# Top-k attention and a gated MLP on one core: low words and signs ahead of the copy of values in ScalarE's queue

## The chip, the cores and the metric

The kernel runs on one core of one Trainium2 chip. A core has a tensor engine (PE in the profile, with its weight loads as PEld), VectorE (DVE), ScalarE (ACT), GpSimd (POOL) and SyncE (SP, which issues the transfers here). Each engine works through its own queue in program order, and semaphores tie the queues together. The metric is the device time of one execution in microseconds, as the median of several runs.

## The reference

```python
# q, k, v: (8, 8, 576, 64) float32; w_in: (512, 2048), w_out: (2048, 512)
scores = scale * np.matmul(q, k.transpose(0, 1, 3, 2))          # (8, 8, 576, 576)
kth = np.partition(scores, -32, axis=-1)[..., -32:-31]
scores = np.where(scores >= kth, scores, -1000000000.0)
attn = np.exp(scores - np.max(scores, axis=-1, keepdims=True))
attn = attn / (np.sum(attn, axis=-1, keepdims=True) + 1e-09)
x = np.matmul(attn, v)            # then (B, H, S, D) -> (4608, 512)
h = x @ w_in
g = h * (1.0 / (1.0 + np.exp(-1.702 * h)))
out = (g @ w_out).astype(np.float32)
```

Every row of scores keeps its 32 largest entries, goes through a softmax and is multiplied by the values. The result goes through two matrix products with a quick GELU between them.
The weights arrive as 64-bit floats: each is one low and one high 32-bit word.

## The kernel before

The work is cut into 144 *slots*; a slot is 128 rows of two heads. Slot n runs a pipeline over neighbouring slots: top-k of slot n on VectorE, the exponentials of slot n-1 on ScalarE, the transposes ("turn") and the products with the values of slot n-2 on PE, and the scores of slot n+2 on PE.

The weights are brought in as 32 pieces of 128 x 512 in the first twelve slots (0 to 11). Each is rebuilt from its two words by five steps on three engines:

```python
raws = pool("raws", 8)            # pieces land here, eight buffers
dgp = pool("dgp", 1)              # diagonals "by", one buffer
ps_t = pool("ps_t", 2, space=PSUM)  # transposes (tp) and values (o) share two buffers

def finish():                     # GpSimd, in the slot behind the piece's own
    nc.gpsimd.tensor_tensor(out=whole, in0=whole, in1=low.bitcast(I32), op=ALU.add)      # L140
    nc.gpsimd.tensor_tensor(out=dst, in0=dst, in1=high, op=ALU.mult)                     # L141
return {
    "size": lambda: nc.scalar.activation(dst, high, AF.Abs, scale=REBASE),               # L144
    "shift": lambda: nc.vector.tensor_scalar(bits, bits, 3, None, op0=ALU.logical_shift_left),  # L145
    "sign": lambda: nc.scalar.activation(high, high, AF.Sign),                           # L146
    "low": lambda: nc.scalar.mul(out=low.bitcast(I32), in_=low, mul=2.0**-29),           # L147
    "finish": finish,
}
```

The fillers are products of the identity that nobody reads. They keep PE busy while there is no MLP work:

```python
def stay_warm(count, of=ident[:]):
    none = ps_p.tile([P, C], F32, name="none", tag="po")
    for i in range(count):
        nc.tensor.matmul(none[:, 0:P], lhsT=of, rhs=of, start=True, stop=True)           # L162
```

One of the first twelve slots in program order (cut; each engine's queue is what it gets of this, in this order):

```python
def slot(n):
    # ... loads for later slots
    some = [round_piece(x) for x in by_slot.get(n, [])] if n else early
    # ... (slot 0 does low and sign here)
    bounds(n - 1)                 # GpSimd: cut, low (L270, L271)
    exponentials(n - 1)           # ScalarE: two Prelu (L279), two Exp (L281), sums into den
    copy_scores(n + 1)            # ScalarE: sc out of PSUM (L242)
    tanh(False)                   # ScalarE, if an MLP block waits (L402)
    if n > 1:
        turn_main(n - 2)          # PE: tp (L312), ScalarE: pt (L320), twice
        turn_ends(n - 2)          # PE: tp (L315), ScalarE: pt
    for piece in some:
        piece["size"]()
    for i, op in enumerate(topk(n)):      # VectorE: eight MAX8 (L251), six MATCH_REPLACE8 (L254)
        op()
        if i == 2:
            for _ in range(min(2, len(unfinished))):
                finish_one()      # GpSimd: two pieces of the slot before
        if i == 5:
            if n > 0:
                divide(n - 1)     # VectorE: some (L290), rden (L292); GpSimd: by (L296), twice
            while unfinished:
                finish_one()      # GpSimd: the pieces left over
        if i == 9:
            gate(False)           # VectorE (L418)
    for piece in some:
        piece["shift"]()
        unfinished.append(piece["finish"])
    if n > PROJECTS and may_project(2):   # PROJECTS = 7
        project(range(G))         # PE: po, four fp32 products (L433), eight rows in the profile
    # ... prepare in slots 0 to 3
    scores(n + 2)                 # PE: s_ps (L231)
    # ...
    idle = not ready and n < PROJECTS
    if idle and n > 1:
        stay_warm(4)
    if n > 1:
        values(n - 2)             # PE: o (L342), ScalarE: xT (L354)
    for piece in some:
        piece["low"]()
    # ... prepare in later slots
    for piece in some:
        piece["sign"]()
    if idle:
        stay_warm(4)
    hidden()                      # PE: one MLP block, ph (L385), if one is ready
```

The slots from 12 on have another order (two at a time), and no pieces and no fillers. The change doesn't touch them.

Of the kernel before, what the change touches and what calls it, by code (L numbers as in the profile page):

```python
# [28 lines left out]
def kernel(  # L29
# [94 lines left out]
    def round_piece(n):  # L124

        c, g = pieces[n]
        dst = wout[:, g, :] if c is None else win[:, c, g * PIECE : (g + 1) * PIECE]
        words = raw.pop(n)[:].rearrange("p (n w) -> p n w", w=2)
        low, high = words[:, :, 0], words[:, :, 1].bitcast(F32)
        bits, whole = dst.bitcast(U32), dst.bitcast(I32)

        def finish():
# [10 lines that stand above are left out]
# [8 lines left out]
# [5 lines that stand above are left out]
# [75 lines left out]
    def copy_scores(n):  # L238
        ps = st[n].pop("ps")
        sc = st[n]["sc"] = scp.tile([P, 2, S], F32, name="sc")  # L240
        for i in range(2):
            nc.scalar.copy(out=sc[:, i, :].rearrange("p (c k) -> p c k", c=2), in_=ps[i][:, :, 0:HALF])  # L242

    def topk(n):

        sc = st[n]["sc"]
        top = st[n]["top"] = small.tile([P, 2, TOPK], F32, name="top")
        left = lefts.tile([P, 2, S], F32, name="left")

        def largest(r, i):  # L250
            nc.vector.max(top[:, i, 8 * r : 8 * r + 8], (left if r else sc)[:, i, :])  # L251

        def remove(r, i):
            nc.vector.match_replace(  # L254
                left[:, i, :], top[:, i, 8 * r : 8 * r + 8], (left if r else sc)[:, i, :], LOWEST
            )

        ops = []
        for r in range(TOPK // 8):
            ops += [lambda r=r, i=i: largest(r, i) for i in range(2)]  # L260
            if r < TOPK // 8 - 1:
                ops += [lambda r=r, i=i: remove(r, i) for i in range(2)]
        return ops

    def bounds(n):

        top = st[n]["top"]
        cut = st[n]["cut"] = small.tile([P, 2], F32, name="cut")
        low = st[n]["low"] = small.tile([P, 2], F32, name="low")
        nc.gpsimd.tensor_scalar(cut[:], top[:, :, TOPK - 1], -1.0, None, op0=ALU.mult)  # L270
        nc.gpsimd.tensor_tensor(out=low[:], in0=top[:, :, TOPK - 1], in1=top[:, :, 0], op=ALU.subtract)  # L271

    def exponentials(n):

        sc, cut, low = st[n]["sc"], st[n]["cut"], st[n]["low"]
        pr = st[n]["pr"] = prp.tile([P, 2 * S], F32, name="pr")
        den = st[n]["den"] = small.tile([P, 2], F32, name="den")
        for i in range(2):
            nc.scalar.activation(sc[:, i, :], sc[:, i, :], AF.Prelu, bias=cut[:, i : i + 1], alpha=HUGE)  # L279
        for i in range(2):  # L280
            nc.scalar.activation(  # L281
                pr[:, i * S : (i + 1) * S], sc[:, i, :], AF.Exp, bias=low[:, i : i + 1],
                accum_out=den[:, i : i + 1],
            )

    def divide(n):

        den, pr = st[n]["den"], st[n]["pr"]
        some = small.tile([P, 2], F32, name="some")
        nc.vector.tensor_scalar_add(some[:], den[:], 1e-9)  # L290
        rden = small.tile([P, 2], F32, name="rden")
        nc.vector.reciprocal(rden[:], some[:])  # L292
        if n < SETTLED:
            by = st[n]["by"] = dgp.tile([P, 2, P], F32, name="by")
            for i in range(2):
                nc.gpsimd.tensor_scalar(by[:, i, :], ident[:], rden[:, i : i + 1], None, op0=ALU.mult)  # L296
        else:
            nc.scalar.activation(pr[:, 0:S], pr[:, 0:S], AF.Copy, scale=rden[:, 0:1])
            nc.gpsimd.tensor_scalar(pr[:, S : 2 * S], pr[:, S : 2 * S], rden[:, 1:2], None, op0=ALU.mult)  # L299
# [22 lines left out]
    def turn_main(n):  # L322
        for i in range(2):
            turn(n, i * NF, MAIN[i], NF)

    def turn_ends(n):

        turn(n, 2 * NF, FULL, 1)
# [68 lines left out]
    def tanh(aside):  # L397

        if to_gate:
            ph, g, rows = to_gate.pop()  # L400
            th = thp.tile([P, G, P], F32, name="th")
            nc.scalar.activation(th[:], ph[:], AF.Tanh, scale=0.851 / RAISE)  # L402
            if aside:
                h = raws.tile([P, G, P], F32, name="h", tag="raw")
                nc.scalar.copy(out=h[:], in_=ph[:])
                ph = h
            gated.append((th, ph, g, rows))

    def gate(aside):
        if not gated:  # L410
            return
        th, h, g, rows = gated.pop()
        gT = gtp.tile([P, G, P], F32, name="gT")
        if aside:
            nc.gpsimd.tensor_scalar(th[:], th[:], 1.0, None, op0=ALU.add)  # L415
            nc.gpsimd.tensor_tensor(out=gT[:], in0=th[:], in1=h[:], op=ALU.mult)  # L416
        else:
            nc.vector.scalar_tensor_tensor(  # L418
                out=gT[:], in0=th[:], scalar=1.0, in1=h[:], op0=ALU.add, op1=ALU.mult
            )  # L420
        to_project.append((gT, g, rows))
# [29 lines left out]
    READY = (((-9, -8), (-7, -6), (-4, -3), (-2, -1)), ((-7, -6), (-4, -3), (-3, -2), (-1, -2)))  # L451
    FETCH = (((-13, -12), (-11, -10), (-7, -7), (-5, -4)), ((-11, -10), (-9, -8), (-5, -5), (-2, -2)))
    VALUES = ((-8, -7, 0, 0), (-8, -7, 2, 2))
    by_slot = dict(enumerate([2, 2, 2, 3, 3, 3, 3, 4, 3, 3, 2, 2]))
    for n in by_slot:
        first = sum(map(len, list(by_slot.values())[:n]))
        by_slot[n] = list(range(first, first + by_slot[n]))
# [19 lines left out]
    def finish_one():  # L477
        unfinished.pop(0)()
        finished.append(None)

    def may_project(waiting):

        return len(to_project) > waiting and len(finished) >= NG * CC + (to_project[0][1] + 1) * G
# [25 lines left out]
    def slot(n):  # L509

        todo = later.pop(n, [])
        for fn, args in todo:
            if fn is not prepare:
                fn(*args)
        preparing = [args for fn, args in todo if fn is prepare]
        some = [round_piece(x) for x in by_slot.get(n, [])] if n else early
        if n == 0:
# [3 lines that stand above are left out]
        else:  # L521
            bounds(n - 1)
            exponentials(n - 1)
            copy_scores(n + 1)
            tanh(False)
            if n > 1:
                turn_main(n - 2)
                turn_ends(n - 2)
            for piece in some:
                piece["size"]()  # L530
        for i, op in enumerate(topk(n)):
# [3 lines that stand above are left out]
                    finish_one()  # L535
            if i == 5:
                if n > 0:
                    divide(n - 1)
                while unfinished:
                    finish_one()  # L540
            if i == 9:
                gate(False)
# [3 lines that stand above are left out]
        if n > PROJECTS and may_project(2):  # L546
            project(range(G))
        if n < NP:
            for args in preparing:
                prepare(*args)  # L550
        scores(n + 2)
        if n == SETTLED:
            copy_scores(n + 2)
        if n == 0:
            return
        idle = not ready and n < PROJECTS
        if idle and n > 1:
            stay_warm(4)
        if n > 1:
            values(n - 2)  # L560
        for piece in some:
            piece["low"]()
        if n >= NP:
            for args in preparing:
                prepare(*args)
        for piece in some:
            piece["sign"]()
        if idle:
            stay_warm(4)
        hidden()  # L570

    def last_slot():
# [115 lines left out]
```

## Time and profile before

The time before is 1635.64 us (median of 3 runs, 1635.34 to 1639.87). The profiled execution has a span of 1639.6 us.

| engine | busy us | share of the span |
|---|---|---|
| PE (matmul) | 1590.0 | 97% |
| PEld (weight load) | 1185.1 | 72% |
| DVE | 1474.0 | 90% |
| ACT | 1153.8 | 70% |
| POOL | 750.7 | 46% |

The shares are averages over two stages. Up to about 173 us the twelve slots with pieces run; behind them come the slots that are all attention and MLP. The engines are read stage by stage below.

How to read the views: a row of the timeline or of the chain of waits begins with its start and its duration in us, then come the engine, the line of the kernel, the operation and the tiles (out<-in). "xN" is a count; an fp32 product shows as two rows, so four fillers are "x8". Text in square brackets is idle time ahead of a row and what ended it. Durations of following rows overlap a little, so a step's cost is taken from start to start. The list of waits gives "who <- whom: us in total, times, longest".

### The profile page before, as it was taken

The numbers are of one execution on the slowest core, as the hardware profiler recorded it, in microseconds if no ns is written. First come the engines' busy times: TensorE is split into PE (matmuls) and PEld (weight loads), VectorE is DVE, ScalarE is ACT, GpSimd is POOL, SyncE is SP. The second block draws the span as 40 slices with busy tenths as digits, with TensorE's granted clock in tenths as the row PEclk, the third lists the DMA queues.
The fourth block names the chain that finished last, engine by engine and source line by source line (L and its number), as shares of the span: only waits on it lengthen the run. The fifth ranks groups of instructions, "written<-read, shape, count | busy, mean of one in ns | idle before, by whom it ended". The sixth has DMA issues, their size and how long they took to land.

```text
span 1639.6 us, 32136 instructions
## 1 busy us (share of the span) xinstructions
PE 1590.0 (97%) x12031; PEld 1185.1 (72%) x12031; DVE 1474.0 (90%) x3213; ACT 1153.8 (70%) x2446; POOL 750.7 (46%) x782
## 2 busy tenths in 40 slices
PE   7678999999999999999999999999999999999999
PEld 5466677777777777777777777777777777777776
DVE  7887899999999999999999998999999999999960
ACT  6786776777777777777777777677777777777761
POOL 3676444444444444444444444444444444444430
PEclk7789999999999999999999999999999999999999
DMA  7232001110001001111000100111000100000000
GB/s 240 93 129 81 22 22 29 29 43 15 23 15 43 23 22 29 29 28 30 13 21 12 37 22 22 30 29 43 15 23 15 44 22 22 22 8 8 8 7 14
DMA packets 100636, 56.61 MB, mean 35 GB/s; under 512 B 83584, under 2 KB 91776, under 8 KB 100480
## 3 DMA queue, kind: packets, MB, share of 16 engines
q1 hardware_dynamic: 100480, 54.55, 11.7%
q8 instruction: 95, 1.56, 0.4%
q14 instruction: 61, 0.50, 0.1%
HBM read 45.09 MB, written 9.44 MB: 33 GB/s over the span
## 4 chain that ended last, share of the span: by engine, by line
PE 91%; ACT 5%; DVE 2%; issue 1%; POOL 0%; DMA 0%; SPq 0%; POOLq 0%; ACTq 0%
PE ph L385 31%; PE po L433 30%; PE s_ps L231 10%; PE o L342 10%; PE tp L310 8%; PE tp L199 2%; ACT sc L242 1%; ACT pr L281 1%; ACT raw L147 1%; ACT raw L146 1%; DVE top L251 1%; DVE left L254 1%; ACT sc L279 0%; PE none L162 0%; PE tp L315 0%
## 5 line engine op out<-in xcount | busy, mean ns | idle before, releaser
L251 DVE MAX8 top<-left 128x8 f32<-128x576 f32 x864 | 609.4, 747 | 0.0
L433 PE MATMUL po<-wout,gT 128*128 128x512 f32 x1152 | 545.2, 598 | 1.9 <-POOL wout L141 1.2
L385 PEld LDWEIGHTS ph<-xT,win 128*128 128x128 f32 x4096 | 467.4, 192 | 40.1 <-issue 39.8
L385 PE MATMUL ph<-xT,win 128*128 128x128 f32 x4096 | 484.5, 277 | 0.0
L254 DVE MATCH_REPLACE8 left<-top,left 128x576 f32<-128x576 f32 x576 | 423.3, 743 | 0.0
L299 POOL TENSOR_SCALAR pr<-pr,rden 128x576 f32<-128x576 f32 x133 | 230.1, 1730 | 348.2 <-ACT th L402 348.2
L433 PEld LDWEIGHTS po<-wout,gT 128*128 128x128 f32 x1152 | 199.1, 192 | 150.1 <-issue 143.3
L415 POOL TENSOR_SCALAR th<-th 128x512 f32<-128x512 f32 x132 | 197.4, 1495 | 228.1 <-ACT th L402 228.1
L320 ACT COPY pt<-tp 128x512 f32<-128x512 f32 (+1 forms) x432 | 193.0, 482 | 149.4 <-PE tp L310 142.7
L279 ACT ACTIVATE sc<-sc,cut 128x576 f32<-128x576 f32 x288 | 208.1, 774 | 116.0 <-POOL cut L270 116.0
L281 ACT ACTIVATE pr<-sc,low 128x576 f32<-128x576 f32 x288 | 219.2, 764 | 0.0
L242 ACT COPY sc<-s_ps 128x576 f32<-128x576 f32 x288 | 169.7, 644 | 69.2 <-PE s_ps L231 69.0
L310 PEld LDWEIGHTS tp<-ident,pr 128*128 128x128 f32 x1197 | 143.2, 141 | 101.9 <-issue 57.2
L254 DVE MATCH_REPLACE8 left<-top,sc 128x576 f32<-128x576 f32 x288 | 211.6, 742 | 0.0
L251 DVE MAX8 top<-sc 128x8 f32<-128x576 f32 x288 | 202.1, 743 | 10.1 <-ACT sc L242 10.1
L231 PE MATMUL s_ps<-k_t,q_t 64*128 64x288 f32 (+1 forms) x1280 | 187.0, 439 | 1.1 <-ACT k_t L201 1.0
L310 PE MATMUL tp<-ident,pr 128*128 128x128 f32 x1197 | 174.1, 273 | 0.0
L416 POOL TENSOR_TENSOR gT<-th,h 128x512 f32<-128x512 f32 x132 | 168.7, 1278 | 11.0
L342 PE MATMUL o<-pt,v_l 128*64 128x128 f32 (+1 forms) x2560 | 159.0, 267 | 0.7
L342 PEld LDWEIGHTS o<-pt,v_l 128*64 128x64 f32 x2560 | 131.6, 138 | 31.9 <-ACT pt L320 13.5
L231 PEld LDWEIGHTS s_ps<-k_t,q_t 64*128 64x128 f32 (+1 forms) x1280 | 101.4, 181 | 63.1 <-issue 43.6
L290 DVE TENSOR_SCALAR some<-den 128x2 f32<-128x2 f32 x144 | 46.3, 322 | 102.2 <-ACT pr L281 102.2
(55 smaller groups left out, 1164.1 us busy)
## 6 DMA issues: line engine op xcount, KB each, us to landing
q_l<-in_q_dram SPq DMA_DIRECT2D x64, 128.0 KB, 2.9
k_l<-in_k_dram SPq DMA_DIRECT2D x64, 128.0 KB, 2.9
raw<-in_moe_w_in_dram SPq DMA_DIRECT2D x16, 512.0 KB, 5.1
v_l<-in_v_dram SPq DMA_DIRECT2D x32, 256.0 KB, 2.9
raw<-in_moe_w_out_dram SPq DMA_DIRECT2D x16, 512.0 KB, 3.3
out_dram<-ob SPq DMA_DIRECT2D x32, 256.0 KB, 2.3
ends<-in_q_dram SPq DMA_DIRECT2D x32, 32.0 KB, 2.4
ends<-in_k_dram SPq DMA_DIRECT2D x32, 32.0 KB, 2.5
```

The source lines that it names most:

```text
L231: nc.tensor.matmul(ps[i][rows, c, 0:HALF], lhsT=qT[b, hps[p]][on, cols], rhs=kT[b, hps[p]][on, FIRST[i] + c * HALF : FIRST[i] + (c + 1) * ...
L251: nc.vector.max(top[:, i, 8 * r : 8 * r + 8], (left if r else sc)[:, i, :])
L254: nc.vector.match_replace(left[:, i, :], top[:, i, 8 * r : 8 * r + 8], (left if r else sc)[:, i, :], LOWEST)
L279: nc.scalar.activation(sc[:, i, :], sc[:, i, :], AF.Prelu, bias=cut[:, i : i + 1], alpha=HUGE)
L281: nc.scalar.activation(pr[:, i * S : (i + 1) * S], sc[:, i, :], AF.Exp, bias=low[:, i : i + 1], accum_out=den[:, i : i + 1],)
L299: nc.gpsimd.tensor_scalar(pr[:, S : 2 * S], pr[:, S : 2 * S], rden[:, 1:2], None, op0=ALU.mult)
L310: nc.tensor.transpose(tp[:, c * P : (c + 1) * P], pr[:, at], ident[:])
L320: nc.scalar.copy(out=to, in_=tp[:, 0 : blocks * P])
L342: nc.tensor.matmul(o[j * D : (j + 1) * D, 0 : cols.stop - cols.start], lhsT=main[:, j, c, :] if c < NF else tail[:, j, :], rhs=pt[:, j * N ...
L385: nc.tensor.matmul(ph[:, i, :], lhsT=win[:, c, f * P : (f + 1) * P], rhs=xT[:, c, :], start=(c == 0), stop=(c == CC - 1),)
L415: nc.gpsimd.tensor_scalar(th[:], th[:], 1.0, None, op0=ALU.add)
L433: nc.tensor.matmul(po[:], lhsT=gT[:, i, :], rhs=wout[:, f, :], start=(f == 0), stop=(f == FC - 1))
```

## The change

Three things change, all in the first twelve slots.

- The low words and the signs of a slot's pieces are issued ahead of values, so in ScalarE's queue they stand ahead of the copy of values (xT), which has to wait for PE. Before, they stood behind it.
- The fillers of PE that stood half ahead of values and half behind it now all stand behind it. (In slot 1, which had only the four behind, there are eight.)
- The pieces are spread anew: slot 2 rounds three in place of two, and slot 7 three in place of four.

```diff
-    by_slot = dict(enumerate([2, 2, 2, 3, 3, 3, 3, 4, 3, 3, 2, 2]))
+    by_slot = dict(enumerate([2, 2, 3, 3, 3, 3, 3, 3, 3, 3, 2, 2]))
@@ slot(n) @@
             return
+        for piece in some:
+            piece["low"]()
+        for piece in some:
+            piece["sign"]()
         idle = not ready and n < PROJECTS
-        if idle and n > 1:
-            stay_warm(4)
         if n > 1:
             values(n - 2)
-        for piece in some:
-            piece["low"]()
         if n >= NP:
             for args in preparing:
                 prepare(*args)
-        for piece in some:
-            piece["sign"]()
         if idle:
-            stay_warm(4)
+            stay_warm(8)
         hidden()
```

The aim is that ScalarE does work that needs nothing from PE while it would otherwise wait for PE, and that values, and with them the next slot's exponentials, come earlier. No arithmetic on the data changes.

## The prediction

> **What bounds the kernel now.** I first read the busy shares and the clock row of the page. Over the whole span the tensor engine is 97% busy, so the question was whether the change touches a stretch where it is not. The pieces of weights are rounded in the first twelve slots only (slots 0 to 11), so I cut the span at the starts of ScalarE's first Prelu in slots 1 and 12 (20.57 and 173.08 us in its timeline). The view of stretches (length; busy PE, PEld, DVE, ACT, POOL; granted clock; DMA share; GB/s):
>
> ```profile
> 20.57:173.08 152.51, 115.42 (x821) 89.06 (x819) 126.56 (x279) 115.27 (x233) 99.62 (x105) 0.84 0.37 123
> 180.30:1639.60 1459.30, 1455.06 (x11132) 1082.98 (x11132) 1329.63 (x2895) 1020.81 (x2174) 641.93 (x660) 1.00 0.09 24
> ```
>
> From 180 us on PE is busy 1455 of 1459 us at full clock: nothing that the change does can shorten that part. In the head no engine is full: DVE, the fullest, works 126.6 of 152.5 us, and PE runs at 0.84 of its clock. So the head is a chain through engines. The chain of waits in slots 3 and 4 shows its links (start, us, engine and tile):
>
> ```profile
> 53.64 0.27 ACT xT L354
> 53.90 1.73 ACT raw L147 x3
> 55.63 1.67 ACT raw L146 x3
> 57.30 0.71 ACT sc L279 x2
> 58.01 0.51 issue
> 58.52 1.63 ACT pr L281 x4
> 60.15 1.06 ACT sc L242 x2
> 61.20 0.49 ACT pt L320
> 61.69 0.04 issue
> 61.74 0.69 PE tp L315 x4
> 62.43 2.22 PE s_ps L231 x8
> 64.65 2.00 PE none L162 x8
> 66.66 1.32 PE o L342 x20
> 67.97 0.02 issue
> 68.00 0.27 ACT xT L354
> ```
>
> Read it as a ring. The copy of values (xT) waits for values (o) on PE. Low words (L147) and signs (L146) stand behind it in ScalarE's queue, though they need nothing from PE. Then come Prelu and Exp, the copies of scores and of pt, and PE again, where four fillers (none) stand ahead of values. One round: 57.30 to 71.67 (the next sc L279 in the chain) is 14.37 us. The list of waits from 40 to 175 us says who sits idle for it (total us, times, longest):
>
> ```profile
> PE tp L315 <- ACT pt L320: 32.6, 9, 5.3
> ACT xT L354 <- PE o L342: 31.6, 8, 6.3
> DVE some L290 <- ACT pr L281: 25.6, 8, 5.1
> ```
>
> ScalarE idles 31.6 us ahead of the copy of values while the low words and signs could run. DVE idles 25.6 us for the exponentials' sums. DVE's own timeline gives what a slot costs it:
>
> ```profile
> 51.44 1.08 DVE L145 TENSOR_SCALAR win<-win 128x512 uint32<-128x512 uint32 x3
> 60.18 0.17 DVE L290 TENSOR_SCALAR some<-den 128x2 f32<-128x2 f32 x1 [3.56 <-ACT pr L281]
> 122.46 3.37 DVE L145 TENSOR_SCALAR wout<-wout 128x512 uint32<-128x512 uint32 x3
> ```
>
> Three shifts take 1.0 us (the next instruction starts at 52.44), and once 3.37 us, while GpSimd works on wout.
>
> **What the Trainium skill says.** "TensorE: Matmul & The Clock Gate", section "Architectural detail: the array is 16× 32×32, not 1× 128×128", calls ScalarE, VectorE and GpSimd strict FIFO. The trace agrees: low words issued behind xT start only after it (53.80 after 53.64), after 4.25 us of idleness. The same page, "What's actually happening", says that an idle window of about 3.4 us halves PE's clock and a busy one restores it. The trace agrees roughly: in slots 3 to 7, behind idle gaps of 2.2 to 5.3 us, eight score matmuls take 2.2 us; behind the gap of 1.94 us at 165 us they take 1.17. "SBUF — State Buffer", section "Who interferes with whom", says that DVE's tensor_scalar in its two-port mode and GpSimd block each other; the 3.37 us above fit that.
>
> **The change, part by part.**
>
> *Order in ScalarE's queue.* For a slot with three pieces the ring loses 1.73 + 1.67 = 3.40 us, since low and sign now run while PE does L315, scores and values. They add no work. ScalarE's own content of a slot becomes its limit: Prelu start to the third pt copy 57.19 to 62.64 = 5.45, sizes 1.72, low 1.73, sign 1.67, xT 0.2: 10.8 us, and 11.3 with the tanh (0.49), from slot 6 on.
>
> *Fillers.* Four fillers ahead of values go: 2.00 us of the ring in slots 2 to 4, somewhat less in slot 5. Eight now follow values. In slot 1 there are eight where four were, at a half-cold clock some 1 to 2 us more of PE. There PE has about 1 us to spare before pt is wanted at 35.06, so I charge 0.2.
>
> *The ring after both.* 14.37 - 3.40 - 2.00 = 8.97 us, shorter than the other limits, so it ceases to bind. What binds instead, for three pieces: DVE: top-k 9.91 (30.95 to 40.86) + shifts 1.00 = 10.9, with the gate (0.59) 11.5. ScalarE 10.8 or 11.3. GpSimd: bounds 0.84, three finishes of 1.37 + 1.26 each 7.9, the two diagonals 1.16: 9.9. So DVE binds, with ScalarE right behind.
>
> *Pieces.* With four pieces slot 7's finishes would keep GpSimd 12.5 us, above DVE; three keep it at 9.9. Slot 2 takes the third piece: ScalarE there ends at about 42.0, as Prelu of slot 3 did (42.16), so it is free. Its load is issued at about 25 us and wanted at 37.5.
>
> *Slots 8 to 10* also hold eight projecting matmuls ahead of scores and values on the ring. Before: 16.65, 16.77 and 15.68 us, with po at 4.9 to 5.4 us because PE had just idled. Minus low and sign (3.4): 13.2. If PE stays warm, its whole content is L315 0.44, po 3.44 (the tail's x8 rows), scores 1.17, values 1.27, ph 3.6, transposes 1.78: 11.7 us, a full engine. I take 12.2 for slot 8 (part cold) and 11.8 for slot 9. In slot 10 the last projecting matmul needs the third finish of slot 9's pieces, which stands behind the diagonals: Prelu + 5.4, + 1.2, + 2.6, + last matmul 0.9, + scores, values and xT 2.7 = 12.8.
>
> The sum, as distances between Prelus of following slots, before and after:
> slot 1 10.57, 10.6; slot 2 11.02, 10.9; slot 3 15.03, 10.9; slot 4 14.37, 11.0; slot 5 14.09, 11.1; slot 6 13.04, 11.8 (DVE 11.5, and the first ph block, which now waits for the late xT copy, pushes transposes by 0.3); slot 7 14.36, 11.7; slot 8 16.65, 12.2; slot 9 16.77, 11.8; slot 10 15.68, 12.8; slot 11 10.93, 11.2 (DVE 9.91 + 0.59 + 0.66).
> Totals 152.5 and 126.0: 26.5 us less. Behind slot 12 PE is full and its work is the same, so this carries to the end: 1635.64 - 26.5 = 1609.1. I add 1 us for frictions: 1610.
>
> **The rivals.** *DVE and GpSimd collide.* Without gaps both are near full, and the shifts may fall on finishes each time: 1.1 us each in place of 0.34, 2.3 us a slot. Against it: GpSimd's 9.9 leaves it a gap of 1 us, which falls where the next top-k ends. If it happens in half of nine slots, +10 us: 1620. *PE stays cold or binds in slots 6 to 10.* With fillers behind values, and ph behind fillers, transposes come later; if po stays at 4.9, slots 8 to 10 cost 13.2 each: +3 us, 1613. *The head's gain is absorbed later*, because PE then waits for DVE or for weights. Against it: DVE is 91% busy behind 180 us and PE had waited there for nothing; the finishes come earlier as well. It would leave 1625 or more; I give it little. *More than my sum:* DVE's gaps (25.6) and its stretched shifts (2.4) are nearly all that the head can give, about 29 us with no stall at all: 1606.5.
>
> **Range and chances.** The floor near 1606 is hard, as DVE's work stays; 0.3 us more in each of nine slots is 1613, 0.8 is 1617. So 1605 to 1617. Two per cent would be 32.7 us, more than DVE's gaps hold: 0.05 for faster by over 2%. Slower by 2% needs a new wait of 60 us: 0.01.
>
> **What would show it.** Right: the waits of DVE on pr and of ScalarE on o fall from 25.6 and 31.6 us to a few; Prelus of slots 3 to 5 stand 10.9 to 11.2 us apart; slot 12's first Prelu starts at about 147; the clock of the head rises above 0.9; the part behind it keeps its length. Wrong: DVE idle for GpSimd or shifts of over 2 us (collision), po at 4.9 us (cold), or PE gaps behind 160 us that were not there.

## The result, and the profile after

The changed kernel takes 1616.31 us (median of 4 runs, 1614.26 to 1616.51). The kernel before, timed with it, takes 1637.76 us (4 runs, 1635.34 to 1641.75). The ratio is 0.9864, with a 95% interval of 0.9839 to 0.9889: 21.4 us less, between 18 and 26 by the interval. The forecast was 1610 us, with a range of 1605 to 1617.

The view of stretches of the changed kernel, cut at the same places as before, the first Prelu of slot 1 and of slot 12 (columns: length; busy PE, PEld, DVE, ACT, POOL; clock; DMA share; GB/s):

```profile
21.80:149.09 127.29, 106.80 (x824) 84.68 (x822) 123.82 (x280) 115.39 (x233) 101.89 (x106) 0.89 0.45 146
156.30:1614.70 1458.40, 1454.20 (x11131) 1082.50 (x11129) 1328.76 (x2893) 1020.88 (x2174) 640.92 (x660) 1.00 0.09 24
```

The head fell from 152.5 to 127.3 us and DVE now works 123.8 of them, 97%. The stretch behind it is as long as it was (1458.4 for 1459.3 us), at full clock and full of PE. The gain was made in the head, and nothing took it back later. In the two traces the first Prelu of slot 1 comes 1.2 us later, slots 1 to 11 take 25.2 us less and slot 12 0.9 us less; together that is the 24.9 us between these two executions (1641.35 and 1616.48 us).

The list of waits from 40 to 149 us has the three rows that carried the prediction, much smaller:

```profile
PE tp L315 <- ACT pt L320: 14.0, 5, 3.6
ACT xT L354 <- PE o L342: 6.7, 3, 3.8
DVE some L290 <- ACT pr L281: 3.0, 2, 2.1
```

ScalarE's waits for values fell from 31.6 to 6.7 us, DVE's for the exponentials from 25.6 to 3.0. The chain of waits of slots 3 and 4 no longer goes round through ScalarE and PE:

```profile
43.18 1.32 DVE top L251 x2
44.49 1.46 DVE left L254 x2
45.95 1.33 DVE top L251 x2
47.28 0.08 DVE some L290
47.36 0.02 issue
47.38 0.15 DVE rden L292
47.53 1.46 DVE left L254 x2
48.99 1.32 DVE top L251 x2
50.31 1.46 DVE left L254 x2
51.77 1.33 DVE top L251 x2
53.09 1.00 DVE win L145 x3
54.09 1.32 DVE top L251 x2
```

One slot of VectorE without a gap: 43.18 to 54.09 is 10.91 us. From slot 8 on PE takes over: its timeline shows no idle time from 104.12 us, ahead of slot 8's projecting matmuls, to 133 us, ahead of the last one of slot 10. The distances between the first Prelus of following slots (read from ScalarE's timeline) compare step by step with the forecast. "Again" is a second execution of the changed kernel, from the runs below.

| slot | before | forecast | changed | again |
|---|---|---|---|---|
| 1 | 10.57 | 10.6 | 10.58 | 10.57 |
| 2 | 11.02 | 10.9 | 10.91 | 11.21 |
| 3 | 15.03 | 10.9 | 10.92 | 10.68 |
| 4 | 14.37 | 11.0 | 10.91 | 10.85 |
| 5 | 14.09 | 11.1 | 10.91 | 10.91 |
| 6 | 13.04 | 11.8 | 12.04 | 11.51 |
| 7 | 14.36 | 11.7 | 10.98 | 11.51 |
| 8 | 16.65 | 12.2 | 13.46 | 11.73 |
| 9 | 16.77 | 11.8 | 11.97 | 11.97 |
| 10 | 15.68 | 12.8 | 13.46 | 13.44 |
| 11 | 10.93 | 11.2 | 11.15 | 11.14 |
| sum | 152.5 | 126.0 | 127.3 | 125.5 |

### The profile page after: what moved, and what is told of

It reads as the page before. It is cut to its first block, busy times and chain, and to the rows that moved or that the text cites. A ratio compares the mean times of both kernels' runs of the same rounds, so it can differ in the third digit from the quotient of the medians.

```text
span 1614.7 us, 32152 instructions
## 1 busy us (share of the span) xinstructions
PE 1583.5 (98%) x12039; PEld 1182.7 (73%) x12039; DVE 1470.4 (91%) x3213; ACT 1153.7 (71%) x2446; POOL 752.0 (47%) x782
## 3 DMA queue, kind: packets, MB, share of 16 engines
q1 hardware_dynamic: 100480, 54.55, 12.2%
## 4 chain that ended last, share of the span: by engine, by line
PE 91%; DVE 5%; ACT 3%; POOL 1%; issue 1%; DMA 0%; SPq 0%; POOLq 0%; ACTq 0%
PE ph L385 31%; PE po L433 30%; PE s_ps L231 10%; PE o L342 10%; PE tp L310 8%; DVE top L251 2%; DVE left L254 2%; PE tp L199 2%; ACT sc L242 1%; ACT pr L281 1%; POOL wout L140 0%; ACT sc L279 0%; DVE win L145 0%; PE tp L312 0%; ACT pt L320 0%
## 5 line engine op out<-in xcount | busy, mean ns | idle before, releaser
L270 POOL TENSOR_SCALAR cut<-top 128x2 f32<-128x2 f32 x144 | 40.3, 280 | 213.0 <-DVE top L251 212.7
```

## The experiments

The theory: the head was bound by a ring from ScalarE through PE back to ScalarE, closed by the order in ScalarE's queue. Once the ring is short, VectorE is the floor, up to slot 7. The rivals: the fillers ahead of values held the ring; GpSimd was overloaded in slot 7; ScalarE's own work is the new floor. The first four runs take the change apart, the next ones load VectorE, and the last ones act on what the changed kernel still waits for.

**Low words and signs alone.** Fillers and pieces stay as before.

```diff
+        for piece in some:
+            piece["low"]()
+        for piece in some:
+            piece["sign"]()
         idle = not ready and n < PROJECTS
         if idle and n > 1:
             stay_warm(4)
         if n > 1:
             values(n - 2)
-        for piece in some: piece["low"]() ...
-        for piece in some: piece["sign"]() ...
```

> Only low words and signs are moved ahead of values; fillers stay half ahead of values, pieces stay as before. Theory (a ring ScalarE - PE - ScalarE bound the head, and DVE binds once it is shorter): the ring of slots 3 and 4 falls from 14.4 by 3.4 to 11.0 us, next to DVE's 10.9, so nearly the whole gain comes from this part: 18 to 21 us less than before. Rival (the fillers ahead of values hold the ring): 10 us less at most, Prelus of slots 3 to 5 still 12.5 us or more apart.

Measured: 1617.68 us (1616.94 to 1619.63), ratio to before 0.9883 (0.9867 to 0.9900). Slots 3 to 5 are 10.91, 11.81 and 10.45 us. By the ratio that is about 19 us less (16 to 22), so this part alone brings most of the gain, with four fillers still ahead of values. The rival of the fillers is out. The order of fillers adds about 1 us to it: the run with the new order and the old pieces, below, differs from this one by the fillers alone, and its four times (1615.35 to 1616.91 us) all lie below the four of this one.

**Fillers alone.**

```diff
         idle = not ready and n < PROJECTS
-        if idle and n > 1:
-            stay_warm(4)
 ...
         if idle:
-            stay_warm(4)
+            stay_warm(8)
```

> Only the fillers are moved behind values. Theory: the ring of slots 3 to 5 loses 1.7 to 2.0 us each and still binds at about 12.4 us: 5 to 6 us less than before, nothing in slots 6 to 10. Rival (fillers ahead of values hold the ring): 10 us or more less. Second rival (PE colder, scores and po slower): 0.

Measured: 1636.26 us (1634.15 to 1639.01), ratio 0.9990 (0.9981 to 1.0000): at most 3 us, where 5 to 6 were expected. What it is compared with matters here. Of the 31 runs of the kernel before that stood beside it, 14 lie between 1635.3 and 1637.5 us and 17 between 1639.9 and 1642.5; 11 of the 12 with the fillers alone lie below 1637.1. In the traces, slots 1 to 11 take 146.4 us, 6.1 less than in the trace that the prediction read (slot 3 12.43 for 15.03, slot 4 13.45 for 14.37, slot 5 13.44 for 14.09, slot 6 11.49 for 13.04) and 3.9 less than in two later traces of the kernel before. Slot 3 came to the 12.4 us expected. The ring of slots 4 and 5 shrank by less, and the chain of waits in slot 4 shows why:

```profile
55.25 0.70 ACT sc L279 x2
55.95 0.53 issue
56.48 1.61 ACT pr L281 x4
58.09 1.05 ACT sc L242 x2
59.14 0.49 ACT pt L320
59.63 0.04 issue
59.68 0.69 PE tp L315 x4
60.37 2.22 PE s_ps L231 x8
62.59 2.38 PE o L342 x20
64.97 0.02 issue
65.00 0.27 ACT xT L354
65.26 1.74 ACT raw L147 x3
67.00 1.70 ACT raw L146 x3
```

The ring is still there, 13.45 us in place of 14.37. The 2.00 us of fillers are gone from it, but values now take 2.38 us where they took 1.32 behind the fillers: the granted clock is 0.50 from L315 to 65.5 us, so it is half for values too. In the kernel before it is half from L315 to 66.6 us, and there the fillers fill that time. In this slot, taking fillers off the path put half of their cost on the products behind them.

**Pieces alone.**

```diff
-    by_slot = dict(enumerate([2, 2, 2, 3, 3, 3, 3, 4, 3, 3, 2, 2]))
+    by_slot = dict(enumerate([2, 2, 3, 3, 3, 3, 3, 3, 3, 3, 2, 2]))
```

> Only the pieces are spread anew, in the order of before. Theory: the ring gets 1.1 us longer in slot 2 and 1.1 us shorter in slot 7: within 1 us of before. Rival (four pieces in slot 7 bind GpSimd before as well): 2 us less.

Measured: 1638.75 us (1637.32 to 1644.09), ratio 1.0000 (0.9989 to 1.0010). Slot 2 grew from 11.02 to 12.15 us, the 1.1 us of the ring. Slot 7 shrank from 14.36 to 13.15, but two later traces of the kernel before have 12.7 us there, so that half of the theory is not shown. Slots 1 to 11 took 152.7 us in sum.

**The new order without the new pieces.** The changed kernel with the list of before, the diff above backwards.

> The changed kernel with the pieces as before (two in slot 2, four in slot 7). Theory: four pieces make ScalarE's slot 7 13.0 us and GpSimd's finishes 12.5 us, slot 2 gets 0.3 us shorter: 1 to 2 us more than the changed kernel, the excess between the Prelus of slots 7 and 9. Rival (the stall at the cold projecting matmuls of slot 8 hides it): no more than the changed kernel.

Measured: 1616.36 us (1615.35 to 1616.91), ratio 0.9873 (0.9857 to 0.9888). It is no slower than the changed kernel, as the rival had it. Slot 7 costs 12.87 us (for 10.98), but slot 8 costs 12.78 (for 13.46), and slots 1 to 3, 6 and 9 together are 1.1 us shorter. With the fuller slot 7, PE idles only 1.51 us ahead of slot 8's projecting matmuls and they take 3.70 us. In the changed kernel it idles 2.61 us and they take 5.40. This compares single traces: the second one of the changed kernel has slots 6 to 8 2.4 us shorter than here, and the changed kernel's own times spread over 3.5 us (1614.19 to 1617.70), more than the 1 to 2 us looked for. The new list of pieces brought nothing that can be measured.

**Each shift in two.** The data stay the same, VectorE has one more short instruction per piece. This in the changed kernel and in the kernel before:

```diff
-"shift": lambda: nc.vector.tensor_scalar(bits, bits, 3, None, op0=ALU.logical_shift_left),
+"shift": lambda: [nc.vector.tensor_scalar(bits, bits, by, None, op0=ALU.logical_shift_left) for by in (1, 2)],
```

> The changed kernel with each shift cut in two (by 1 and by 2 bits), so VectorE has 0.34 us more per piece and the data stay the same. Theory (VectorE is the floor of slots 1 to 7 of the changed kernel): 22 pieces of slots 0 to 7 add 7.5 us, those of slots 8 to 11 little, as VectorE has 3 us of idle time there: 7 to 9 us more than the changed kernel, the Prelus of slots 3 to 6 11.9 us apart in place of 10.9. Rival (ScalarE's own work, or its ring with PE, is the floor there): less than 3 us more.

> The same doubling in the kernel before. Theory (the ring hides VectorE from slot 3 on): only slots 0 to 2 pay, 1 to 2.5 us more than before. Rival (VectorE was as much the limit before): 7 us or more.

Measured: 1656.38 us (1653.15 to 1656.47) and 1655.69 us (1653.05 to 1656.37), ratios to before 1.0103 (1.0080 to 1.0127) and 1.0102 (1.0083 to 1.0122). The changed kernel lost 40 us where 7 to 9 were expected, the kernel before 18 where 1 to 2.5 were. VectorE's and GpSimd's timelines in the changed kernel so loaded, where slot 3's shifts meet the finishes of its pieces:

```profile
60.98 5.48 DVE L145 TENSOR_SCALAR win<-win 128x512 uint32<-128x512 uint32 x6
```

```profile
61.98 1.34 POOL L140 TENSOR_TENSOR win<-win,raw 128x512 int32<-128x512 int32 x1
63.40 1.35 POOL L141 TENSOR_TENSOR win<-win,raw 128x512 f32<-128x512 f32 x1
64.71 1.46 POOL L140 TENSOR_TENSOR win<-win,raw 128x512 int32<-128x512 int32 x1
```

Six shifts should take 2.0 us. The first ones do, up to 61.98, when GpSimd starts on the finishes; from there on each shift lasts until one of GpSimd's steps ends. So the load was not 1.0 but 4.4 us a slot. All of it shows in the Prelu distances of the changed kernel, 15.3 us in slots 3 to 5 for 10.9, so VectorE is on the path there.

In the kernel before, the same load filled VectorE's gaps first. Its idle time ahead of L290, 3.56 and 3.13 us in the top-k's of slots 4 and 5, is gone; from the start of one top-k to the next they take 15.32 and 15.35 us, for 14.78 and 14.38 without the load. VectorE's timeline, first the shifts of slot 4, then the addition in slot 5's top-k:

```profile
72.61 5.49 DVE L145 TENSOR_SCALAR win<-win 128x512 uint32<-128x512 uint32 x6
82.13 0.14 DVE L290 TENSOR_SCALAR some<-den 128x2 f32<-128x2 f32 x1
```

So the ring had hidden 3.9 and 3.4 of the 4.4 us there. On ScalarE slots 3 to 5 took 15.25, 14.44 and 14.13 us, nearly what they were, as ScalarE still had a lead to lose; slots 1 and 2 had paid, and slots 6 and 7 did, where VectorE with the load (15.9 us) is longer than the ring. Slots 8 and 10 grew too. By the sizes that were written down the rival was met in the kernel before (7 us or more), as the load came out four times as large as meant. With it VectorE is 99% busy in slots 1 to 10 of both kernels, and both take the same time, 1656 us: where VectorE is full, the order in ScalarE's queue brings nothing.

**One more MAX8 per slot.** A cleaner load on VectorE, its result unused.

```diff
+        nc.vector.max(spare[:], st[n]["sc"][:, 0, :])
         for piece in some:
             piece["shift"]()
```

> The changed kernel with one more MAX8 of 0.66 us behind each top-k of slots 0 to 11, its result unused: VectorE work that, unlike a shift, GpSimd does not hold up. Theory (VectorE is the floor of slots 1 to 7): eight slots of 0.66 us, 5 to 6 us more than the changed kernel, Prelus of slots 3 to 6 11.6 us apart. Rival (ScalarE's 10.8 us or its ring is the floor): 11.0 apart, under 2 us more.

Measured: 1631.91 us (1631.39 to 1633.33), ratio 0.9961 (0.9948 to 0.9975): 15.6 us more than the changed kernel in place of 5 to 6. Slots 4 and 5 are 12.55 us, so 1.64 us came from 0.66. The rest is in VectorE's timeline, with GpSimd's row beside it:

```profile
62.09 1.14 DVE L292 TENSOR_SCALAR some<-den 128x2 f32<-128x2 f32 x1
```

```profile
61.92 1.29 POOL L141 TENSOR_TENSOR win<-win,raw 128x512 f32<-128x512 f32 x1
```

The addition on 128 x 2 values (L290 of the other kernels) takes 0.15 us in the changed kernel. Here it falls into a finish and ends with it. The chain of waits of slot 3 is VectorE alone (spare, win, top, left, some, top again), so it is the floor. Twice a load on it cost more than itself, as it shifted the instructions that cannot run beside GpSimd.

**Warm fillers, and finishes first.** The changed kernel had two things left, in slots 8 and 10. In slot 8 PE's clock drops just then; the view of stretches (length; busy PE; clock; DMA share; GB/s) of the changed kernel:

```profile
102.00:104.00 2.00, 0.00 (x0) 1.00 0.58 158
104.00:105.00 1.00, 0.88 (x5) 1.00 0.99 316
105.00:106.00 1.00, 1.00 (x3) 0.57 1.02 220
106.00:107.00 1.00, 1.00 (x2) 0.50 0.75 194
107.00:108.00 1.00, 1.00 (x2) 0.50 0.73 299
108.00:109.00 1.00, 1.00 (x3) 0.73 0.06 16
109.00:110.00 1.00, 1.00 (x5) 1.00 0.47 94
```

PE works again from 104.1 us on, but the clock is halved from 105.1 to 108.5 (cut into stretches of 0.1 us), while the projecting matmuls run. In slot 10 the last of them waits for the third finish, which stands behind the diagonals in GpSimd's queue. Two edits, the first alone, then both:

```diff
             stay_warm(8)
         hidden()
+        if n in (6, 7):
+            stay_warm(8)
```
```diff
-            for _ in range(min(2, len(unfinished))):
+            for _ in range(min(3, len(unfinished))):
```

> The changed kernel with eight more fillers behind the MLP block of slots 6 and 7, so PE idles 0.7 in place of 2.6 us ahead of slot 8. Theory (an idle gap of 2.6 us halves PE's clock just when slot 8 projects): po of slot 8 3.7 in place of 5.4 us, the Prelus of slots 8 and 9 about 11.8 in place of 13.5 us apart, 1 to 1.7 us less. Rival (the fillers delay the transposes, or po is held by the weights' last step): no gain.

> As the run with warm fillers, and all three finishes of GpSimd stand ahead of the diagonals. Theory (slot 10 waits for the third finish behind the diagonals): the idle 1.2 us of po in slot 10 goes and its Prelu distance falls from 13.5 to about 11.9 us, another 1.2 to 1.6 us less. Rival (late diagonals hold up the transposes): no gain or a loss.

> The changed kernel again, as the measure for the two runs ahead: 1616 us, within 1 us.

Measured: fillers 1615.36 us (1614.58 to 1616.01), both 1613.40 us (1612.52 to 1613.90), the changed kernel 1615.99 us (1614.19 to 1617.70); ratios to before 0.9858 (0.9841 to 0.9874), 0.9845 (0.9829 to 0.9862) and 0.9865 (0.9844 to 0.9886). PE's timeline of slot 10, in the first trace of the changed kernel, then with both edits:

```profile
130.12 2.84 PE L433 MATMUL po<-wout,gT 128*128 128x512 f32 x6
134.19 1.12 PE L433 MATMUL po<-wout,gT 128*128 128x512 f32 x2 [1.22 <-POOL wout L141]
```

```profile
128.24 3.70 PE L433 MATMUL po<-wout,gT 128*128 128x512 f32 x8
```

Slot 10 falls from 13.46 to 11.96 us, as the theory has it. Slot 12 gives 0.7 us back (13.19 for 12.45 us in the second execution of the changed kernel). With both edits slots 1 to 11 take 124.1 us. The runs with both all lie below those of the changed kernel; their intervals against before overlap, and the gain is 2.6 us by the medians. Slot 8 took 11.7 us in both traces with the fillers, but also in the second execution of the changed kernel, without them, its gap being 1.53 us. There the clock's drop fell one slot earlier, on values and the MLP block of slot 7 (half from 93.6 to 96.9 us), which held nothing up. So that loss comes in some executions only, and the fillers alone show no gain beyond the spread. In their own trace VectorE met GpSimd's finishes in slots 6 and 7:

```profile
84.78 1.59 DVE L145 TENSOR_SCALAR wout<-wout 128x512 uint32<-128x512 uint32 x3
90.40 1.15 DVE L290 TENSOR_SCALAR some<-den 128x2 f32<-128x2 f32 x1
```

These two slots took 24.55 us there for 23.02 in both traces of the changed kernel, nearly as much as slot 8 gained.

**The kernel before, profiled twice more.** The runs of the kernel before lie between 1635.3 and 1642.5 us, most of them near 1636.5 or 1641.5, and the trace that the prediction read was of one at 1641.35.

> The kernel before, looked at once more. Its runs lie near 1636.5 or near 1641.5 us, and the profile that the prediction read was of one at 1641. Theory: the 5 us lie in the head, where PE's clock drops behind idle gaps at the ring, so in an execution near 1636.5 one or two of the slots 2 to 6 are 2 to 3 us shorter with scores or transposes at full clock, and the part behind slot 12 is the same. Rival: they lie in the part behind slot 12, or ahead of slot 1.

> The kernel before, a third look, for an execution near 1636.5 us. Theory (the spread of the kernel before lies in PE's clock at the ring of the head): slots 1 to 11 take 147 to 149 us in place of 152.5, with fewer products at half clock, and the rest is as it was. Rival: slots 1 to 11 take 152 us again and another part is shorter.

Measured: 1639.85 and 1639.96 us; neither was near 1636.5. Both have 150.3 us for slots 1 to 11, 2.2 less than the first trace (slot 3 13.7 for 15.0 us, slot 7 12.7 for 14.4, slot 6 13.9 for 13.0), while Prelus of slots 12 to 14 lie as far apart as they did and slot 1's first Prelu comes 0.7 to 0.8 us later. So the 1.5 us between these executions and the first lie in the head. Where the executions near 1636.5 save theirs was not seen and stays open.

## Why the prediction came out as it did

- **The bound** was read rightly. That the ring through ScalarE's queue held slots 3 to 10 is shown by the run with low words and signs alone, where slots 3 to 5 and 8 to 10 are 2.2 to 4.8 us shorter each. For slots 6 and 7 it shows less: 24.8 us together, for 26.6 to 27.4 in the traces of the kernel before. That VectorE did not hold slots 4 and 5 is shown by the 3.4 to 3.9 us of it that the kernel before hid there.
- **The new floor**, VectorE's 10.9 us, came out: 10.91 or 10.92 in slots 2 to 5, and both loads on VectorE show in the Prelu distances. The collision with GpSimd, a rival in the forecast, hardly came in the changed kernel: three shifts took 1.0 to 1.1 us. But it came in both loads on VectorE, and in single slots of the runs with low words and signs alone (L290 1.10 us in slot 6) and with warm fillers. That the changed kernel was spared it is in part luck.
- **The step on fillers** had the wrong size. It took 2.00 us off the ring; alone the part took 0.9 off slot 4 and 0.65 off slot 5, as values then ran at half clock. In the whole change this cost nothing, since the ring no longer bound.
- **The step on pieces** held for slot 2 in the old order; for slot 7 it is not shown. For the new order I had expected four pieces to cost what GpSimd and ScalarE exceed VectorE by. In its trace they cost 1.9 us in slot 7, and the neighbouring slots gave that back.
- **Slots 8 and 10** were 1.3 and 0.7 us longer than forecast. In slot 8 "part cold" was too little: the drop of the clock hit the projecting matmuls in full (5.40 us, for 3.70 when warm). This was one of the signs of being wrong that the forecast names (po at 4.9 us). In another execution it did not come there, and the slot took 11.73. Slot 9 is PE's own work without a gap, 11.97 for a forecast of 11.8. In slot 10 the wait for the third finish was the right step; it was 0.7 us too short.
- **The signs** mostly came: the waits fell, slots 3 to 5 are 10.91 us, the part behind the head kept its length. The clock of the head rose to 0.89 and not above 0.9, and slot 12's first Prelu starts at 149.1 us (146.8 in the second execution) for 147.
- **The sum** for slots 1 to 11 was 126.0 us, measured 127.3 and 125.5. But 26.5 us were taken off 1635.64, the median then, though the 152.5 us belonged to an execution at 1641.35. From that one to the profiled one of the changed kernel (1616.48) the difference is 24.9 us; between the medians it is 21.4. Taken off 1641.35, the same sum gives 1615.9 with its 1 us of friction. So the term that was mis-sized is, as far as the traces go, the head before: in an execution near the median it is probably shorter than in the trace read. The two later traces point that way, with 2.2 us less in the head at 1.5 us less in all. The full 5 us were not seen in a trace. The measured 1616.31 us lies 0.7 us inside the upper end of the range.

## What to carry to other kernels

In a queue that runs in order, put work that waits for nobody ahead of the instruction that waits for another engine, above all when that instruction closes a ring between two engines; here two moved loops brought about 19 us (16 to 22), the fillers about 1 us on top of that, and the new list of pieces nothing that could be told from zero. Take a ring's length from the chain of waits, subtract what leaves it, and compare it with each engine's own work in the slot: the largest of these is a first estimate of the new distance. Take the base of a forecast from the execution whose profile is read, not from the median of others.

## What was not expected of the hardware

A VectorE instruction that cannot run beside GpSimd's is held for as long as GpSimd's lasts, however small it is: an addition on 128 x 2 values took 1.14 us in place of 0.15, and 1.0 us of extra shifts lengthened the slot by 4.4 us. This agrees with the Trainium skill, "SBUF — State Buffer", section "Who interferes with whom", which says that the second of the two to come is blocked for the whole of the other's instruction. In the timeline the time counts as VectorE's busy time, so the list of waits does not show it.

PE's clock can drop after the idle time is over. In slot 8 of the changed kernel, after 2.61 us of idleness, it was still full for 1.0 us of new work and then half for 3.4 us. The length of the gap does not decide it alone: a gap of 2.23 us (slot 6 of the kernel before) was followed by half clock at once, while one slot earlier in the same trace PE idled 2.69 us, and the clock stayed full throughout the work that followed. Gaps of 1.32, 1.51 and 1.53 us ahead of slot 8's matmuls, in other traces, had no drop either.

```profile
93.10 0.44 PE L315 MATMUL tp<-by,pr 128*64 128x128 f32 x4 [2.69 <-ACT pt L320]
93.47 1.24 PE L231 MATMUL s_ps<-k_t,q_t 64*128 64x288 f32 x8
104.12 0.44 PE L315 MATMUL tp<-by,pr 128*64 128x128 f32 x4 [2.61 <-ACT pt L320]
104.49 5.40 PE L433 MATMUL po<-wout,gT 128*128 128x512 f32 x8
```
